# Two unread products behind a LayerNorm, and the Gelu products one V step sooner, in a grouped-query attention and token-mixer decode kernel

## The chip, the cores and the metric

One Trainium2 chip, one of its cores. The metric is the device time of one execution in microseconds; the kernel before has 2511.02 us as the median of three runs (2510.0 to 2511.93).

## The reference, cut to what matters

Two layers, each an attention block over a key/value cache and then a token mixer with a hidden width of 1792 for one token. Batch 2, 8 key/value heads with 4 query heads each, 32768 cached positions of 128 values, model width 512, all in float32. Both layers read the same caches and the same weights, so the caches (1.06 GB for the two layers, less what is kept on chip) pass through the core twice.

```
x = x + A(layernorm(x))      # q = x @ wq; softmax(q k^T * Dh**-0.5) v; @ wo
x = x + B(layernorm(x))      # gelu(h outer w1 + b1) contracted with w2, + b2
x = x + A(layernorm(x))
x = x + B(layernorm(x))
```

In `B` the layernorm's 512 values each meet 1792 hidden units: `u[d, f] = gelu(h[d] * w1[f] + b1[f])`, `y[d] = sum over f of u[d, f] * w2[f] + b2`. The hidden units lie as 14 tiles of 128 partitions by 512 columns.

## The kernel before, in words

**Units and steps.** A unit is (layer, batch, key/value head); there are 32. A unit has a K phase (scores) and a V phase (weighted sum), each of 64 groups of 512 columns, which are worked off four at a time: 16 steps a phase, 1024 steps in all, numbered from 0 in the order that `Order` writes out by hand. A group of the cache fills one of 106 cells of 128 x 512 float32 (256 KB) in SBUF. A step is four matmuls of 128 x 512 into four column strips of one PSUM bank (`k_step` L335, `v_step` L388).

**Hooks.** Everything else is hung on a step: `at(p, f, ...)` (L698) puts a function behind step p, and the loop at the end emits step, hooks, then the loads that may begin after that step. Each engine runs its instructions in the order emitted. So the order of the work on TensorE is written out by hand, and what a hook waits for holds up the V or K steps emitted behind it.

**Loads.** `plan_loads` (L113) decides, from the steps' order and from the microseconds that the hooks are said to take (`us=`, summed by step in `busy`), which cells each load fills, how many groups it has, and the step after which it is issued. All loads go through the queue of SyncE (`load`, L807). A load waits for the steps that last read its cells.

**The change of layer.** A unit of layer 1 needs x after the mixer of layer 0 of its batch. For batch 0 the last unit of layer 0 is x0 = (0, 0, 7), followed in V order by a filler unit of the other batch; then comes y0 = (1, 0, 7), the first unit of layer 1, whose V cells are x0's, still on chip (all 64), with the first 10 groups of K. Batch 1 does the same later with (0, 1, 7), a filler, and (1, 1, 7). While 64 + 10 cells are kept, the filler's V is streamed through 16 cells: four loads of four cells, in turn. Each of them is issued when the step four before it has been worked off.

Behind the last V step of such a unit, called e (e = 463 for the first change, 559 for the second), stand:

- e, e+1: the sum of the heads (`out_1`, `out_2`), `take_rows`
- e+2: `mix_2` (L485, residual into one bank; LayerNorm on VectorE and GpSimd, L492 to L497), `half_way` (`columns`, L552, and L558), ScalarE's table for Gelu
- e+4 to e+11: `hidden_tiles(key, k)` for k = 0 to 7 (L515). Call k first has TensorE multiply the two Gelu tiles of call k-1 (`project`, L507), then ScalarE make tiles 2k and 2k+1 (L522). Of the two tile buffers each is used again only when its product is done.
- e+11: `take_rows` (L465); e+12: `change_1` (x of the new layer, wide query products L300, sum for the mean L546, query row copied by ScalarE L574); e+13: `change_2` (sum of squares L546, power on GpSimd L580, narrow query products L307)
- e+16: the last V step of the filler, then K of the new unit

A third place with the same list, without `half_way`, `change_1` and `change_2`, is the last unit of batch 0 in layer 1, (1, 0, 0), at e = 975, where the steps behind e are K steps. There `mix_4` (L533) follows, which also issues the output's DMA from ScalarE.

**The end.** The last unit, (1, 1, 0), has a tail of its own (`last_rows`, `last_mixer`), with products of TensorE that nobody reads: `unread(n, count)` (L591) multiplies a column of ones with n columns of the tile S into a PSUM bank of the pool `pmisc`. `pmisc` has two banks, in turn used by all small products (`misc` in the profile). A tile of a pool keeps its bank until the last instruction in the program that touches the tile.

Of the kernel before, what the change touches and what calls it, by code (L numbers as in the profile page):

```python
# [13 lines left out]
P = 128  # L14
G = 512
# [180 lines left out]
def gqa_mixer_kernel(ctx: ExitStack, tc: tile.TileContext, x, kt, v, wqo, cols, out):  # L196
    nc = tc.nc
# [5 lines left out]
    FT = (cols.shape[1] - 1) // 3  # L203
# [3 lines left out]
    order = Order(HKV)  # L207
# [14 lines left out]
    def cells(a, n):  # L222
        return mem[:, a * G : (a + n) * G]
# [5 lines left out]
    ident = const.tile([P, P], F32, name="ident")  # L229
    one = const.tile([P, 1], F32, name="one")  # L230
# [7 lines left out]
    S = [const.tile([P, G], F32, name=f"S{k}") for k in range(2)]  # L238
# [349 lines left out]
    rest = [None, None]  # L588
    idle = []

    def unread(n, count=1):  # L591

        if not idle:
            idle.append(pmisc.tile([P, G], F32, name="misc"))
        for _ in range(count):
            nc.tensor.matmul(idle[0][:1, :n], one, S[0][:, :n], start=True, stop=True)  # L596

    def last_rows(u):
        layer, b, h = u
# [13 lines left out]
    def last_mixer(u):  # L613
        layer, b, h = u
        key = (layer, b)
        w = D // 2
        tiles = [cells(tail_at + k, 1) for k in range(TAIL_CELLS)]
        flat, y, few = tiles[FT + 1], tiles[FT + 2], tiles[FT + 3][:, :DH]
        p = px[key]
        st = work.tile([P, 6], F32, name="ln_st")  # L620
        mv = work.tile([P, 2], F32, name="ln_mv")
        rs = work.tile([P, 1], F32, name="ln_rs")
        nc.vector.tensor_copy(few, thin[:, :DH])
        asb["thin"] = few
        out_1(u)
        for k in range(2):
            for r in range(R):
                nc.tensor.matmul(  # L628
                    rest[k][32 * r : 32 * r + 1, :w],
                    oT[u][:, r : r + 1],  # L630
                    wo_of(u)[:, r, k * w : (k + 1) * w],
                    start=True,
                    stop=True,
                )
        unread(P)
        nc.vector.tensor_copy(y[:, :w], rest[0][:, :w])
        nc.scalar.activation(y[:, w:], rest[1][:, :w], AF.Copy)
        nc.tensor.matmul(p, sel1, y, start=False, stop=True, skip_group_check=True)  # L638
        nc.vector.bn_stats(st, p)  # L639
        res = rows[b][:, :P]  # L640
        for g in range(NG):
            nc.tensor.matmul(
                rows[b][32 * g : 32 * g + 1, :P],
                selg[:, 0:1],
                y[:, g * P : (g + 1) * P],
                start=False,
                stop=False,
                skip_group_check=True,
            )
        unread(G, 2)  # L650
        nc.vector.bn_aggr(mv, st)
        deviation(rs, mv)
        off = work.tile([P, 1], F32, name="off", bufs=1)
        nc.vector.tensor_scalar_mul(off, mv[:, 0:1], -1.0)
        nc.vector.tensor_copy(flat, p)
        scale = work.tile([P, FT], F32, name="scale", bufs=1)
        bias = work.tile([P, FT], F32, name="bias", bufs=1)
        nc.vector.tensor_scalar_mul(scale, w1c, rs)
        nc.vector.scalar_tensor_tensor(bias, scale, off, b1c, op0=ALU.mult, op1=ALU.add)

        def project_last(f):
            for g in range(NG):
                nc.tensor.matmul(  # L663
                    rows[b][32 * g : 32 * g + 1, :P],
                    w2c[:, f : f + 1],
                    tiles[f][:, g * P : (g + 1) * P],
                    start=False,
                    stop=(f == FT - 1),
                    skip_group_check=True,
                )  # L670

        for f in range(DIRECT):
            nc.scalar.activation(  # L673
                tiles[f], flat, AF.Gelu_apprx_tanh, bias=bias[:, f : f + 1], scale=scale[:, f : f + 1]
            )
            project_last(f)
            unread(P)
        f0 = DIRECT
        for m in TAIL_GROUPS:
            for f in range(f0, f0 + m):  # L680
                nc.vector.tensor_scalar(
                    tiles[f], flat, scale[:, f : f + 1], bias[:, f : f + 1], op0=ALU.mult, op1=ALU.add
                )
            t = cells(tail_at + f0, m)
            nc.scalar.activation(t, t, AF.Gelu_apprx_tanh)  # L685
            for f in range(f0, f0 + m):
                project_last(f)
            if m == max(TAIL_GROUPS):
                unread(P)
            f0 += m  # L690
        assert f0 == FT
        o = tiles[FT][:, :P]
        nc.vector.tensor_scalar_add(o, res, b2c)
        nc.sync.dma_start(out[b : b + 1, :].rearrange("o (g c) -> (o g) c", g=NG), o[0 : P : P // NG, :])
# [16 lines left out]
    for u in order.units:  # L711
        layer, b, h = u
# [5 lines left out]
        us = (u, mate) if b == 0 and mate not in made and (layer == 0 or h < HKV - 2) else (u,)  # L718
# [5 lines left out]
    for name, us in users.items():  # L724
        k0 = min(first["K", u] for u in us)
        h = name if isinstance(name, int) else name[1]
        layer = min(u[0] for u in us)
        weights.append((k0 - 24 if k0 else -1, (layer, h), max(end["V", u, 1] for u in us) + 3))

    for u in order.units:  # L730
        layer, b, h = u
        key = (layer, b)
        k_mid, k_end = end["K", u, 0], end["K", u, 1]
        v0, v_mid, v_end = first["V", u], end["V", u, 0], end["V", u, 1]
        ahead = order.v_before[u]
# [12 lines left out]
        at(v0 - 1 if u == order.last else v_mid + 2, denominators, u, us=0.4)  # L748
        if u == order.last:
            at(v0 - 1, take_rows, key)  # L750
            at(v0 - 1, table, AF.Gelu_apprx_tanh)
            at(v0 - 1, mix_1, key)
            at(v0 - 1, last_rows, u)
            at(v_mid, unread, G, 3)
            at(v_mid + 4, unread, P, 2)
            at(v_end - 2, take_out, u)
            at(v_end - 2, unread, G)
            at(v_end - 1, out_sum, u)
            at(v_end, last_mixer, u)
            continue  # L760
        at(v_end, take_out, u)
        if u != order.last_of[key]:
            late = 0 if u == order.v_before[order.last] else 1
            at(v_end + late, out_1, u, us=1.2)
            at(v_end + 2 * late, out_2, u, us=2.0)
            continue
        e = v_end
        at(e - 2, mix_1, key, us=1.2)
        at(e, out_1, u, us=1.9)
        at(e + 1, out_2, u, us=2.0)  # L770
        at(e + 1, take_rows, key)
        at(e + 2, mix_2, key, us=1.2)
        if layer == 0:
            at(e + 2, half_way, key, us=1.0)
        at(e + 2, table, AF.Gelu_apprx_tanh)
        for k in range(FT // 2 + 1):
            at(e + 4 + k, hidden_tiles, key, k, us=1.2)
        e += 4 + FT // 2
        at(e, take_rows, key)
        at(e, table, AF.Exp)  # L780
        if layer == 1:
            at(e + 1, mix_4, key, us=1.2)
            continue
        (y,) = [y for y, (x, _) in changed.items() if x == u]
        at(e + 1, change_1, key, y, us=2.2)
        at(e + 2, change_2, key, y, us=0.8)
        assert e + 2 < first["K", y]
# [86 lines left out]
```

## Time and profile before

| what | value |
|---|---|
| median of three runs | 2511.02 us (2510.0 to 2511.93) |
| the profiled execution's own time | 2512.67 us |
| its span, first to last instruction | 2511.0 us |
| granted TensorE clock, mean | 0.754 |
| bytes read | 1064.33 MB, 424 GB/s over the span |

A row of the timeline gives the start in microseconds from the span's start, the duration, the engine, the line, what is written and read, the shape, the number of records, and in brackets the idle time before it and what ended that. A float32 matmul shows as two records, so a V step of four matmuls is "x8". A row of a table by window gives the window, its length, the busy time of the five engines (with counts), the granted clock of TensorE as a share of full speed, the busy share of the 16 DMA engines and the GB/s moved. A row of a DMA issue by line gives the count, the size and the time from issue to landing.

### The profile page before, as it was taken

The numbers are of one execution on the slowest core, as the hardware profiler recorded it, in microseconds if no ns is written. First come the engines' busy times: TensorE is split into PE (matmuls) and PEld (weight loads), VectorE is DVE, ScalarE is ACT, GpSimd is POOL, SyncE is SP. The second block draws the span as 40 slices with busy tenths as digits, with TensorE's granted clock in tenths as the row PEclk, the third lists the DMA queues.
The fourth block names the chain that finished last, engine by engine and source line by source line (L and its number), as shares of the span: only waits on it lengthen the run. The fifth ranks groups of instructions, "written<-read, shape, count | busy, mean of one in ns | idle before, by whom it ended". The sixth has DMA issues, their size and how long they took to land. (4 is left out here: it accounts for less than half of the span.)

```text
span 2511.0 us, 20944 instructions
## 1 busy us (share of the span) xinstructions
PE 1392.1 (55%) x9580; PEld 395.3 (16%) x9580; DVE 179.7 (7%) x486; ACT 186.2 (7%) x580; POOL 5.1 (0%) x18
## 2 busy tenths in 40 slices
PE   3455555554555545556775775455554545555557
PEld 1111111111111111111121121111111111111112
DVE  1000000000000000000010010000000000000011
ACT  0100000000000000001110100000000000000021
POOL 0000000000000000000000000000000000000000
PEclk9777776777767777778887887777677776677788
DMA  9999999999999999999999999999999999999996
GB/s 418 431 431 428 433 434 432 433 433 434 434 433 424 432 435 433 414 433 420 392 421 427 396 428 429 431 433 433 434 434 433 433 424 441 433 426 434 425 432 275
DMA packets 32641, 1065.68 MB, mean 424 GB/s; under 512 B 3877, under 2 KB 3881, under 8 KB 5034
## 3 DMA queue, kind: packets, MB, share of 16 engines
q1 hardware_dynamic: 32264, 1064.32, 98.8%
q8 instruction: 75, 1.23, 0.2%
q14 instruction: 12, 0.10, 0.0%
q10 hardware_dynamic: 290, 0.03, 0.0%
HBM read 1064.33 MB, written 0.00 MB: 424 GB/s over the span
## 5 line engine op out<-in xcount | busy, mean ns | idle before, releaser
L335 PE MATMUL scores<-mem,qz 128*32 128x512 f32 x4096 | 614.6, 740 | 553.2 <-DMA mem<-in_kt_dram 553.2
L388 PE MATMUL acc<-mem,S 128*16 128x512 f32 x4080 | 591.4, 713 | 534.4 <-DMA mem<-in_v_dram 529.4
L370 ACT ACTIVATE S<-S,neg 128x128 f32<-128x128 f32 x256 | 129.9, 510 | 2242.8 <-DVE S L365 1203.9
L335 PEld LDWEIGHTS scores<-mem,qz 128*32 128x32 f32 x4096 | 138.9, 130 | 963.0 <-issue 487.3
L388 PEld LDWEIGHTS acc<-mem,S 128*16 128x16 f32 x4080 | 125.3, 106 | 855.8 <-issue 776.6
L345 DVE TENSOR_REDUCE mx<-scores 128x1 f32<-128x512 f32 x64 | 44.2, 691 | 851.9 <-PE scores L335 851.9
L427 PEld LDWEIGHTS misc<-selg,row 128*128 128x128 f32 x256 | 48.9, 285 | 48.2 <-issue 36.8
L365 DVE STREAM_TRANSPOSE S<-scores 128x512 f32<-128x512 f32 x64 | 45.4, 710 | 113.7 <-PE acc L388 113.7
L427 PE MATMUL misc<-selg,row 128*128 128x4 f32 x256 | 51.7, 325 | 3.3 <-DVE row L419 3.3
L451 PE MATMUL rows<-mem,oT 128*1 128x512 f32 x248 | 51.6, 921 | 0.3 <-DVE oT L442 0.3
L370 ACT ACTIVATION_READ_ACCUMULATOR S<-S,neg 128x1 f32 x256 | 47.8, 187 | 0.0
L355 DVE TENSOR_REDUCE m<-misc 1x4 f32<-1x128 f32 x32 | 8.9, 279 | 367.1 <-PE misc L353 367.1
L419 DVE COPY row<-acc 128x512 f32<-128x512 f32 x32 | 22.1, 691 | 177.3 <-PE acc L388 177.3
L413 DVE RECIPROCAL rl<-misc 128x4 f32<-128x4 f32 x32 | 5.8, 182 | 367.5 <-PE misc L411 367.5
L442 DVE TENSOR_TENSOR oT<-misc,rl 128x4 f32<-128x4 f32 x32 | 5.2, 161 | 270.6 <-PE misc L427 270.2
L507 PE MATMUL rows<-row,cols_sb 128*1 128x512 f32 x42 | 22.3, 614 | 0.6 <-ACT row L522 0.6
L507 PE MATMUL rows<-hid,cols_sb 128*1 128x512 f32 x42 | 22.3, 613 | 0.0
L411 PEld LDWEIGHTS misc<-both,one 128*128 128x128 f32 x64 | 13.7, 267 | 49.7 <-issue 46.8
L300 PE MATMUL misc<-mem,xw 128*32 128x512 f32 x144 | 19.7, 619 | 2.4 <-DVE xw L276 1.9
L522 ACT ACTIVATE row<-bcast,bias,scale 128x512 f32<-128x512 f32 x21 | 16.3, 777 | 39.2 <-PE rows L507 20.6
L307 PEld LDWEIGHTS misc<-selg,row 128*128 128x128 f32 x128 | 16.3, 199 | 17.7 <-issue 10.1
L307 PE MATMUL misc<-selg,row 128*128 128x2 f32 (+1 forms) x128 | 17.7, 260 | 0.8 <-DVE row L292 0.8
(117 smaller groups left out, 240.8 us busy)
## 6 DMA issues: line engine op xcount, KB each, us to landing
mem<-in_kt_dram SPq DMA_DIRECT2D x23, 2048.0 KB, 14.2
mem<-in_v_dram SPq DMA_DIRECT2D x37, 1024.0 KB, 8.8
mem<-in_kt_dram SPq DMA_DIRECT2D x8, 4096.0 KB, 23.8
mem<-in_wqo_dram SPq DMA_DIRECT2D x14, 2048.0 KB, 33.4
mem<-in_v_dram SPq DMA_DIRECT2D x7, 4096.0 KB, 22.9
mem<-in_v_dram SPq DMA_DIRECT2D x3, 6144.0 KB, 30.0
mem<-in_kt_dram SPq DMA_DIRECT2D x18, 1024.0 KB, 10.7
mem<-in_v_dram SPq DMA_DIRECT2D x6, 2048.0 KB, 26.3
```

Source lines behind the costliest of these rows:

```text
L300: nc.tensor.matmul(q_ps[us][32 * d : 32 * d + 32, :], xw[:, d, :], wq[:, d, :], start=True, stop=True)
L307: nc.tensor.matmul(pt[:, r * n : (r + 1) * n], q_row[us][:, r * DH : (r + 1) * DH], side, start=True, stop=True,)
L335: nc.tensor.matmul(sc_ps[u, half][32 * row : 32 * row + 32, :], qz[:, at : at + 32], cells(at_cell["K", u, g], 1), start=(i == 0), stop=(i ...
L345: nc.vector.tensor_reduce(mx[u][:, half : half + 1], sc_ps[u, half], axis=AX.X, op=ALU.max)
L365: nc.vector.transpose(S[half], sc_ps[u, half])
L370: nc.scalar.activation(s[:, :, h], s[:, :, h], AF.Exp, bias=neg[u][:, h : h + 1], scale=SCALE, accum_out=lsum[u][:, half, h : h + 1],)
L388: nc.tensor.matmul(acc[32 * row : 32 * row + R * QT, :], S[half][:, col : col + R * QT], vc, start=(g < NG), stop=(g >= quads - NG),)
L419: nc.vector.tensor_copy(asb[u], acc)
L427: nc.tensor.matmul(po_of[u][:, :R], asb[u][:, t * DH : (t + 1) * DH], selg[:, t * R : (t + 1) * R], start=(t == 0), stop=(t == QT - 1 and ...
L451: nc.tensor.matmul(rows[b][32 * r : 32 * r + 1, :], oT[u][:, r : r + 1], wo_of(u)[:, r, :], start=(u == order.first_of[layer, b]), stop=(u ...
L507: nc.tensor.matmul(rows[key[1]][32 * g : 32 * g + 1, :], w2c[:, f : f + 1], hid.pop((key, f)), start=(f < NG), stop=(f >= FT - NG),)
L522: nc.scalar.activation(hid[key, f], px[key], AF.Gelu_apprx_tanh, bias=shift[key][:, f : f + 1], scale=slope[key][:, f : f + 1],)
```

## The change

- `unread` gets the unit as its first argument. For a unit other than the last it takes a new `misc` tile each time and multiplies the ones with a broadcast column of the identity matrix in place of S.
- In layer 0 two calls are added: 256 columns behind e+2 (after `mix_2`, `half_way` and the table), 512 columns behind e+3.
- `hidden_tiles(key, k)` moves from step e+4+k to e+3+k, in all three places. All that is counted from there (`take_rows`, the table for Exp, `change_1`, `change_2`, `mix_4`) moves one step forward with it, and so do the entries of `busy` that the planner reads.
- For the last unit, a new tile is taken only when the list `idle` is empty, which it is not any more: the tile of the second change of layer serves again.

```diff
-    def unread(n, count=1):
-
-        if not idle:
+    def unread(u, n, count=1):
+
+        if not idle or u != order.last:
+            idle.clear()
             idle.append(pmisc.tile([P, G], F32, name="misc"))
         for _ in range(count):
-            nc.tensor.matmul(idle[0][:1, :n], one, S[0][:, :n], start=True, stop=True)
+            nc.tensor.matmul(idle[0][:1, :n], one, S[0][:, :n] if u == order.last else ident[:, :1].to_broadcast([P, n]), start=True, stop=True)
...
         at(e + 2, table, AF.Gelu_apprx_tanh)
+        if layer == 0:
+            at(e + 2, unread, u, G // 2)
+            at(e + 3, unread, u, G)
         for k in range(FT // 2 + 1):
-            at(e + 4 + k, hidden_tiles, key, k, us=1.2)
-        e += 4 + FT // 2
+            at(e + 3 + k, hidden_tiles, key, k, us=1.2)
+        e += 3 + FT // 2
         at(e, take_rows, key)
```

The calls of `unread` in the tail pass `u` and are otherwise as they were.

More of the change, by code (lines that the diff above doesn't have):

```diff
@@ L634, in last_mixer @@
                 )
-        unread(P)
+        unread(u, P)
         nc.vector.tensor_copy(y[:, :w], rest[0][:, :w])
@@ L649, in last_mixer @@
             )
-        unread(G, 2)
+        unread(u, G, 2)
         nc.vector.bn_aggr(mv, st)
@@ L676, in last_mixer @@
             project_last(f)
-            unread(P)
+            unread(u, P)
         f0 = DIRECT
@@ L688, in last_mixer @@
             if m == max(TAIL_GROUPS):
-                unread(P)
+                unread(u, P)
             f0 += m
@@ L753, in gqa_mixer_kernel @@
             at(v0 - 1, last_rows, u)
-            at(v_mid, unread, G, 3)
-            at(v_mid + 4, unread, P, 2)
+            at(v_mid, unread, u, G, 3)
+            at(v_mid + 4, unread, u, P, 2)
             at(v_end - 2, take_out, u)
-            at(v_end - 2, unread, G)
+            at(v_end - 2, unread, u, G)
             at(v_end - 1, out_sum, u)
```

## The prediction

> **What bounds the kernel.** I read the page first, then windows around the two changes of layer, then the timeline and the SyncE queue there and at the end.
>
> ```profile
> span 2511.0 us, 20944 instructions
> ...
> q1 hardware_dynamic: 32264, 1064.32, 98.8%
> ...
> L335 PE MATMUL scores<-mem,qz 128*32 128x512 f32 x4096 | 614.6, 740 | 553.2 <-DMA mem<-in_kt_dram 553.2
> L388 PE MATMUL acc<-mem,S 128*16 128x512 f32 x4080 | 591.4, 713 | 534.4 <-DMA mem<-in_v_dram 529.4
> ```
>
> The load queue is busy 98.8% of the span, and TensorE's idle time before K and V steps ends with a landing. So the time is bytes over the queue's rate plus the tail; an edit on TensorE counts only where it makes a load late. At most 1.2% is to be had, and most of that lies in a few places. Two are the ends of the changes of layer (last two columns: DMA share, GB/s):
>
> ```profile
> 1198.00:1210.00 12.00, 10.53 (x74) 3.27 (x66) 1.78 (x8) 5.49 (x8) 0.00 (x0) 1.00 1.01 421
> 1210.00:1222.00 12.00, 10.56 (x81) 3.95 (x80) 1.81 (x8) 0.00 (x0) 0.54 (x1) 0.86 0.87 326
> 1397.00:1409.00 12.00, 9.25 (x65) 3.33 (x65) 2.43 (x12) 4.79 (x7) 0.54 (x1) 1.00 1.01 420
> 1409.00:1421.00 12.00, 11.63 (x87) 3.73 (x86) 1.15 (x4) 0.00 (x0) 0.00 (x0) 0.86 0.89 335
> ```
>
> Against the 12 us before, 12 x (1 - 326/421) = 2.7 us of transfer are missing at the first change and 12 x (1 - 335/420) = 2.4 us at the second: 5.1 us in all, 0.2% of the time. This is also about what a measurement of this kernel can tell from no change.
>
> Why they are missing, at the first change:
>
> ```profile
> 1202.58 1.05 PE L388 MATMUL acc<-mem,S 128*16 128x512 f32 x8 [0.21 <-DMA mem<-in_v_dram]
> ...
> 1205.05 1.05 PE L388 MATMUL acc<-mem,S 128*16 128x512 f32 x8 [0.50 <-DMA mem<-in_v_dram]
> 1206.04 1.05 PE L552 MATMUL misc<-selg,row 128*128 128x1 f32 x8
> 1207.35 1.06 PE L300 MATMUL misc<-mem,xw 128*32 128x512 f32 x8 [0.26 <-DVE xw L566]
> 1208.34 0.38 PE L546 MATMUL misc<-xw,one 128*128 128x4 f32 x2
> 1208.66 1.05 PE L388 MATMUL acc<-mem,S 128*16 128x512 f32 x8
> 1209.64 0.39 PE L546 MATMUL misc<-sq,one 128*128 128x4 f32 x2
> 1211.43 1.15 PE L307 MATMUL misc<-pair,row 128*128 128x1 f32 x8 [1.40 <-DVE pair L584]
> 1212.51 4.27 PE L388 MATMUL acc<-mem,S 128*16 128x512 f32 x24
> ```
>
> Steps e+11 and e+12 come 2.47 us apart, with the landings. `change_1` puts e+13 at 1208.66, `change_2` puts e+14 at 1212.51, though its load landed about 2.5 us before. The queue meanwhile (an issue, then its size and time to landing, from windows around that issue alone):
>
> ```profile
> 1209.77 0.33 SPq L807 DMA_DIRECT2D mem<-in_kt_dram  x1
> mem<-in_kt_dram SPq DMA_DIRECT2D x1, 512.0 KB, 6.4
> 1214.48 0.33 SPq L807 DMA_DIRECT2D mem<-in_kt_dram  x1
> mem<-in_kt_dram SPq DMA_DIRECT2D x1, 1024.0 KB, 6.3
> 1407.06 0.33 SPq L807 DMA_DIRECT2D mem<-in_kt_dram  x1
> mem<-in_kt_dram SPq DMA_DIRECT2D x1, 512.0 KB, 6.4
> 1411.20 0.33 SPq L807 DMA_DIRECT2D mem<-in_kt_dram  x1
> mem<-in_kt_dram SPq DMA_DIRECT2D x1, 1024.0 KB, 5.9
> 1437.29 0.33 SPq L807 DMA_DIRECT2D mem<-in_kt_dram  x1
> mem<-in_kt_dram SPq DMA_DIRECT2D x1, 2048.0 KB, 8.1
> ```
>
> The load behind e+13 has only 2 groups (512 KB), that behind e+14 has 4. The second is issued at 1214.48, 1.97 us after e+14 began, and lands at 1220.8, the one ahead of it at 1216.2: 4.6 us for 2.47 us of data, 2.2 us lost. A late load takes 6.3 - 2.5 = 3.8, 5.9 - 2.5 = 3.4 or 8.1 - 4.9 = 3.2 us beyond its data (0.61 us a group). I call this the lead: a load is in time when issued some 3.5 us before the load ahead of it lands.
>
> **The change, part by part.**
>
> *Unread products.* The nearest row is the tail's own:
>
> ```profile
> 2479.23 2.74 PE L596 MATMUL misc<-S,one 128*1 128x512 f32 x6
> 1185.00:1188.00 3.00, 2.22 (x12) 0.29 (x16) 0.00 (x0) 0.00 (x0) 0.00 (x0) 0.50 1.00 415
> ```
>
> Three of 512 columns take 2.74 us, so 0.9 us one, 0.45 us one of 256, twice that at half clock: 1.4 to 2.7 us of TensorE at each change. The steps e+3 to e+5 wait for landings, and a load there may be issued over 3 us late before the queue runs dry, since four loads circulate (4 x 2.47 less the lead and a step). Cost 0; were that cover gone, up to 2.7 us. The window shows half clock there before the change, with the DMA share at 1.00: what the products may do to the clock is worth 0 as well.
>
> *Products one step sooner.* Call 0's two Gelu tiles follow the LayerNorm at once in either version, since ScalarE does not wait for TensorE there; the products follow e+4 in place of e+5. From then on each call keeps pace with the landings, so `take_rows`, `change_1` and `change_2` come 2.47 us sooner. The moved steps issue no load and change no order on the SyncE queue; GpSimd's power and the Exp table go with them, with nothing of other units in between. The output's DMA of `mix_4` moves one K step, in a stage where the queue is full.
>
> `change_2` does not get shorter: what it delays is now e+13 in place of e+14. First change: e+13 at 1212.51 - 2.47 = 1210.04, its 512 KB load issued 1.97 us later at 1212.0. The load ahead of it, the filler's last, lands at 1206.17 + 8.8 = 1215.0 now, and does so still, though it is issued about 1 us later behind a later e+12:
>
> ```profile
> 1206.17 0.33 SPq L807 DMA_DIRECT2D mem<-in_v_dram  x1
> mem<-in_v_dram SPq DMA_DIRECT2D x1, 1024.0 KB, 8.8
> ```
>
> The lead is 3.0 us, so 0.5 us is lost, and some 0.4 us by the load after it. Against 2.2 us (2.7 us with what trails) the gain is 1.3 us; I take **-1.5**, between -2.7 and 0.
>
> Second change, where the chain has one wait more. `misc` has two banks, but the tile taken behind e+3 here is used again in the tail, so its bank is held from here to the end and all small products share one:
>
> ```profile
> 1404.63 1.06 PE L300 MATMUL misc<-mem,xw 128*32 128x512 f32 x8 [0.26 <-DVE xw L566]
> 1405.63 0.38 PE L546 MATMUL misc<-xw,one 128*128 128x4 f32 x2
> 1405.77 0.60 ACT L574 ACTIVATE row<-misc 128x512 f32<-128x512 f32 x1 [3.50 <-PE misc L300]
> 1409.67 4.46 PE L388 MATMUL acc<-mem,S 128*16 128x512 f32 x24
> ```
>
> L546's sum stood beside L300's bank; now it waits until ScalarE has copied that at 1406.37: 0.7 us on `change_1`, and step e+12 and `change_2` behind it on TensorE. In the rest of layer 1 each small product begins after the reader of the one before has ended, so nothing is added. Step e+13 then starts at 1409.67 - 2.47 + 0.7 = 1407.9, its load goes out 1.5 us later (1411.20 - 1409.67) at 1409.4. The load ahead lands at 1407.06 + 6.4 - 1.2 = 1412.2 (two groups before the one issued at 1407.06): a lead of 2.8 us, so 0.7 us lost and 0.5 us by the next. That is 1.2 us, and 1.2 us is lost there now (1411.20 + 5.9 = 1417.1 against 1413.5 + 2.47). I take **-0.2**, between -2.4 and +0.7.
>
> Both use the half clock at which these steps run now (0.86 granted in both windows). At full clock the releases come 0.9 us sooner and both changes gain about 1 us more. By the Trainium skill ("TensorE: Matmul & The Clock Gate", "Part 1: The HAM clock gate (the "warmup" mystery)") the clock is halved after an idle window of some 3.4 us that runs free of the kernel's start. By that rule an execution may meet either clock here, and the sum would lie up to 2 us lower; the trace shows half clock at both, so the sum keeps it.
>
> *The planner.* Its list, worked through with the shifted entries, is the same for 213 loads, both changes of layer included, and differs at the end, through the third place (e = 975). Groups, and the step after which they are issued:
>
> | | before | after |
> |---|---|---|
> | V of (1,1,1) | 0-23: 981, 24-31: 983, 32-63: 990 | 0-23: 975, 24-31: 983, 32-55: 983, 56-63: 999 |
> | V of the last unit | 0-15 and 16-31: 999, 32-47: 1007, rest: 1011 | 0-15: 1000, 16-31: 1006, 32-47: 1011, rest: 1015 |
>
> The first half of this gets earlier, the second half later: one step 1000, one 1006, then a step four later for all that is left.
>
> ```profile
> 2425.10 0.33 SPq L807 DMA_DIRECT2D mem<-in_v_dram  x1
> mem<-in_v_dram SPq DMA_DIRECT2D x1, 27.7
> 2452.84 3.61 PE L388 MATMUL acc<-mem,S 128*16 128x512 f32 x16 [16.54 <-DMA mem<-in_v_dram]
> 2472.36 1.06 PE L388 MATMUL acc<-mem,S 128*16 128x512 f32 x8
> 2476.04 0.33 SPq L807 DMA_DIRECT2D mem<-in_v_dram  x1
> ```
>
> Now the load of 32 groups lands at 2452.8, and step 1000 starts on it. With 24 groups that is 8 x 0.61 = 4.9 us sooner, 2447.9; the step at half clock ends near 2449.9 (two take 3.61), and the load behind it is issued at 2450.0, 2.8 us ahead of the landing of the last 8 groups: 0.7 us late. The stage up to step 1008 is 4.9 us sooner too (2467.5), step 1011's load is issued 3.7 us after that (2476.04 - 2472.36) at 2471.2, while the load ahead lands at 2452.8 + 0.7 + 32 x 0.61 = 2473.0: a lead of 1.8 us, 1.7 us late. The rest is in time. Together 2.4 us; the bounds are 0 and 4.5 us: with 3.8 us of lead the two cost 1.0 + 2.0, and if part of steps 1008 to 1011 ran at half clock, 1.5 us more. Some may be made up in the last 64 groups; I take **+2.0**, nearer to the rows than either end.
>
> *Sum:* -1.5 - 0.2 + 2.0 = +0.3 us. The profiled execution (2512.67 us, span 2511.0) lies 1.65 us over the median; the sum is a difference and is laid on the median: **2511.3 us**.
>
> **The rivals.**
>
> *The queue stays full.* If 2 us of lead are enough, none of the loads above is late but the one behind 1011, by 0.2 us (2.0 - 1.8): both shortfalls go and the end costs nothing, 2511.0 - 5.1 + 0.2 = 2506.1, or 2507.8 if only the late loads' own 2.2 + 1.2 us return. For it: 1215.0 - 1212.0 = 3.0 is not far from 3.2. Against it: the load at 1411.20 was issued 2.3 us ahead of the landing at 1413.5 and still lost 1.2. Chance 0.2. The Trainium skill ("SBUF — State Buffer", "The DMA setup-cost knee (why "@ 1 MiB" ≠ asymptote)") gives a transfer a fixed cost of about 2 us; by that the time would be this rival's, and the three late loads above do not agree with it.
>
> *Slower: the last loads.* The place is steps 1000 to 1015. If steps 1008 to 1011 run at half clock (two in 3.61 us, so 7.2 us in place of 3.7), the load behind 1011 goes out at 2474.7, after the one ahead has landed: 5.3 us late, +6.0 at the end, and with nothing gained at the changes 2517.0. It decides from about 2.7 us of delay in that stage on. Against it: the stage is at full clock now, right from 2472. Chance 0.12.
>
> *It does nothing.* The stalls move by one step and the late loads at the end are made up: 2511.0. Chance 0.13; the forecast has 0.55.
>
> **The numbers.** The range reaches to the better half of the first rival, 2507.5, and to 2515.0, where +4.5 at the end meets small gains. Faster by over 0.2% (under 2506.0) needs both shortfalls whole: 0.05. Slower by over 0.2% (over 2516.0): 0.08. The rest, 0.87, is the same.
>
> **What would show it.** Step e+13 in place of e+14 should follow L307; at the second change L546 should start as L574 ends. The windows after 1210 and 1409 should show 350 to 400 GB/s. In the last 60 us there should be a dip of the DMA share near 2452 and 2473, and the last landing near 2493 to 2495. Wrong would be: another plan of loads, a full share at the end, or a landing lead under 2.5 us.

## The result, and the profile after

The changed kernel takes 2514.89 us (median of 13 runs, 2512.39 to 2520.6). Beside it, the kernel before had 2508.85 us (median of 13 runs, 2504.36 to 2511.93). The ratio is 1.0025 with a 95% interval of 1.0017 to 1.0032, so the changed kernel is 6.0 us slower. The forecast was 2511.3 us, 0.3 us more than before and no change that can be told. The time lies inside the stated range of 2507.5 to 2515.0 us, but only by luck: the range was laid on 2511.02 us, and the kernel before was 2.2 us faster in these runs. Taken as differences from before, the range was -3.5 to +4.0 us, and the measured +6.0 us lies outside it.

One thing has to be known for all that follows. The execution profiled before took 2512.67 us, which is 3.8 us above the median of these 13 runs; the one profiled after took 2514.98 us, which is its median. A single profile shows where a wait is; the ratios over many runs say what it is worth. One thousandth is 2.5 us.

The page of the changed kernel, the lines that answer to those shown of before:

```profile
span 2513.3 us, 20953 instructions
...
q1 hardware_dynamic: 32408, 1064.32, 98.8%
...
L335 PE MATMUL scores<-mem,qz 128*32 128x512 f32 x4096 | 612.0, 737 | 555.4 <-DMA mem<-in_kt_dram 555.3
L388 PE MATMUL acc<-mem,S 128*16 128x512 f32 x4080 | 601.2, 721 | 521.2 <-DMA mem<-in_v_dram 516.4
```

The bound is the same: the load queue moves the same bytes and is busy 98.8% of a longer span. TensorE's V products take 601.2 us against 591.4 at the same count and its K products 612.0 against 614.6; the clock granted over the whole span is 0.754 in both, so the clock has to be looked at place by place. The table by window at the two changes of layer (the last three columns: granted clock, DMA share, GB/s):

```profile
1198.00:1210.00 12.00, 8.95 (x65) 3.51 (x60) 2.51 (x13) 3.73 (x6) 0.54 (x1) 1.00 1.01 423
1210.00:1222.00 12.00, 11.09 (x84) 3.17 (x83) 1.16 (x4) 0.00 (x0) 0.00 (x0) 0.86 0.95 346
1397.00:1409.00 12.00, 9.71 (x52) 4.48 (x56) 2.06 (x13) 0.60 (x1) 0.54 (x1) 0.59 0.85 343
1409.00:1421.00 12.00, 10.57 (x80) 3.04 (x76) 0.85 (x2) 0.00 (x0) 0.00 (x0) 0.84 0.79 279
```

At the first change the shortfall is a little smaller than before (346 GB/s for 326). At the second it spreads over both windows: 12 x (1 - 343/421) + 12 x (1 - 279/421) = 2.2 + 4.0 = 6.3 us of transfer are missing, where before it was 2.4. And TensorE has a clock of 0.59 there, in a window in which it had 1.00.

The timeline of the second change in the changed kernel shows why. Two rows of before come first, for comparison: the filler's sum of its two halves on VectorE (L410) and its product on TensorE (L411).

```profile
1382.03 0.15 DVE L410 TENSOR_TENSOR both<-lsum 128x4 f32<-128x4 f32 x1
1399.26 0.38 PE L411 MATMUL misc<-both,one 128*128 128x4 f32 x2
```

```profile
1395.80 0.69 DVE L465 COPY row<-rows 128x512 f32<-128x512 f32 x1 [16.31 <-PE rows L507]
1396.40 0.15 DVE L410 TENSOR_TENSOR both<-lsum 128x4 f32<-128x4 f32 x1
1396.61 0.38 PE L411 MATMUL misc<-both,one 128*128 128x4 f32 x2 [0.89 <-DVE both L410]
1396.93 1.05 PE L388 MATMUL acc<-mem,S 128*16 128x512 f32 x8
...
1399.22 1.94 PE L300 MATMUL misc<-mem,xw 128*32 128x512 f32 x8 [0.26 <-DVE xw L566]
1401.22 0.60 ACT L574 ACTIVATE row<-misc 128x512 f32<-128x512 f32 x1 [5.29 <-PE misc L300]
1401.87 0.59 PE L546 MATMUL misc<-xw,one 128*128 128x4 f32 x2 [0.72 <-ACT row L574]
1402.39 1.91 PE L388 MATMUL acc<-mem,S 128*16 128x512 f32 x8
...
1406.14 1.86 PE L307 MATMUL misc<-pair,row 128*128 128x1 f32 x8 [1.31 <-DVE pair L584]
1407.93 6.01 PE L388 MATMUL acc<-mem,S 128*16 128x512 f32 x32
```

Three things are to be seen.

- **A new wait, 0.89 us.** Before, VectorE did L410 at 1382.03, long ahead, and L411 ran without a wait. Now L410 stands behind the copy of `take_rows` (L465), which itself waited for the last Gelu product. TensorE waits for L410, and the V step of 1396.93 stands behind L411 on TensorE.
- **The held bank, 0.72 us.** L546 waits for ScalarE's copy (L574), as the prediction had it.
- **The clock.** L300, which took 1.06 us before, takes 1.94, and the V step and L307 behind it are as slow (1.91 and 1.86). Before, the whole chain ran at full clock and only the steps behind it at half. The slow stretch begins at L300, behind the wait of 0.89 us and ahead of that of 0.72 us, so in this execution the held bank did not bring it on.

The loads show what this did to the queue. The filler's last V load is issued behind the V step of 1402.39, at 1404.36, and lands 4.6 us later, at 1408.9 (its rows stand in the last section). The next one, the K load of 512 KB behind step e+13, is issued here:

```profile
1409.90 0.33 SPq L811 DMA_DIRECT2D mem<-in_kt_dram  x1
```

That is 1.0 us after the load ahead of it has landed. The prediction had it 2.8 us ahead of that landing.

At the end of the kernel, the window that holds the first late load, the late load itself, and the two waits of TensorE for the last V loads:

```profile
2448.00:2452.00 4.00, 2.63 (x16) 0.49 (x16) 0.00 (x0) 0.00 (x0) 0.00 (x0) 0.50 0.55 233
```

```profile
2451.34 0.33 SPq L811 DMA_DIRECT2D mem<-in_v_dram  x1
...
2472.02 0.33 SPq L811 DMA_DIRECT2D mem<-in_v_dram  x1
mem<-in_v_dram SPq DMA_DIRECT2D x1, 4096.0 KB, 13.1
```

```profile
2474.61 5.15 PE L388 MATMUL acc<-mem,S 128*16 128x512 f32 x32 [2.63 <-DMA mem<-in_v_dram]
...
2485.28 4.94 PE L388 MATMUL acc<-mem,S 128*16 128x512 f32 x32 [2.95 <-DMA mem<-in_v_dram]
```

The load behind step 1011 goes out at 2472.02, 2.6 us ahead of the landing (2474.61, where TensorE's wait ends) of the load in front of it, and takes 13.1 us. The plan of loads is the one that was forecast.

### The profile page after: what moved, and what is told of

The parts are those of the page before. It is cut to its first block, busy times and chain, and to the rows that moved or that the text cites. A ratio compares the mean times of both kernels' runs of the same rounds, so it can differ in the third digit from the quotient of the medians.

```text
span 2513.3 us, 20953 instructions
## 1 busy us (share of the span) xinstructions
PE 1401.5 (56%) x9588; PEld 399.0 (16%) x9588; DVE 179.8 (7%) x486; ACT 186.1 (7%) x580; POOL 5.1 (0%) x18
## 3 DMA queue, kind: packets, MB, share of 16 engines
q1 hardware_dynamic: 32408, 1064.32, 98.8%
## 5 line engine op out<-in xcount | busy, mean ns | idle before, releaser
L335 PE MATMUL scores<-mem,qz 128*32 128x512 f32 x4096 | 612.0, 737 | 555.4 <-DMA mem<-in_kt_dram 555.3
L388 PE MATMUL acc<-mem,S 128*16 128x512 f32 x4080 | 601.2, 721 | 521.2 <-DMA mem<-in_v_dram 516.4
L300 PE MATMUL misc<-mem,xw 128*32 128x512 f32 x144 | 20.5, 645 | 2.4 <-DVE xw L276 1.9
L411 PEld LDWEIGHTS misc<-both,one 128*128 128x128 f32 x64 | 13.6, 265 | 51.2 <-issue 43.9
L307 PEld LDWEIGHTS misc<-selg,row 128*128 128x128 f32 x128 | 16.3, 200 | 19.0 <-issue 8.5
L411 PE MATMUL misc<-both,one 128*128 128x4 f32 x64 | 16.4, 326 | 3.7 <-DVE both L410 3.7
```

The lines of the kernel that those rows point to most:

```text
L300: nc.tensor.matmul(q_ps[us][32 * d : 32 * d + 32, :], xw[:, d, :], wq[:, d, :], start=True, stop=True)
L307: nc.tensor.matmul(pt[:, r * n : (r + 1) * n], q_row[us][:, r * DH : (r + 1) * DH], side, start=True, stop=True,)
L335: nc.tensor.matmul(sc_ps[u, half][32 * row : 32 * row + 32, :], qz[:, at : at + 32], cells(at_cell["K", u, g], 1), start=(i == 0), stop=(i ...
L388: nc.tensor.matmul(acc[32 * row : 32 * row + R * QT, :], S[half][:, col : col + R * QT], vc, start=(g < NG), stop=(g >= quads - NG),)
L411: nc.tensor.matmul(pl[:, :R], ones, both, start=True, stop=True)
```

## The experiments

Each result is the ratio to the kernel before that was measured beside it, with its 95% interval. The intervals are 0.0008 to 0.0013 to either side, so most differences between two kernels lie within them; what is read from such a difference rests on its coming out twice and on the profiles.

The change has five parts that can be set apart: the unread products; the bank that their tile keeps to the end; the earlier products in layer 0; the order on VectorE that comes with them; and the third place, in layer 1, whose only effect on the loads is another plan for the end. The first four kernels take the change apart roughly, the next four one part each.

**e1_move_only.** The products one step sooner in all three places, no unread products ahead of the Gelu tiles; both banks stay free. The cut is against the kernel before.

```diff
-            at(e + 4 + k, hidden_tiles, key, k, us=1.2)
-        e += 4 + FT // 2
+            at(e + 3 + k, hidden_tiles, key, k, us=1.2)
+        e += 3 + FT // 2
```

> The products come one step sooner in all three places, without the two unread products at the changes; the tail takes its own tile, so two banks serve the small products throughout. If the move itself costs (the copy of the rows now stands ahead of the filler's denominators on VectorE, TensorE waits for them at step e+10, and the change runs at half clock): 4 to 6 us over before, like the changed kernel. If the bank held from the second change on is the cost: within 1.5 us of before. If the plan of the last loads is the cost: 1 to 2.5 us over before.

Measured: 1.0034 (1.0021 to 1.0047), from six runs. The move alone, without held bank and without unread products, is slower than before, by 8.5 us and so by more than the 4 to 6 us that were expected.

**e2_unread_only.** The changed kernel with the products at their old steps: unread products and held bank are left.

```diff
-            at(e + 3 + k, hidden_tiles, key, k, us=1.2)
-        e += 3 + FT // 2
+            at(e + 4 + k, hidden_tiles, key, k, us=1.2)
+        e += 4 + FT // 2
```

> The two unread products and the tile reused in the tail, with the Gelu products at their old steps; the plan of loads is that of before. If the move costs: within 1.5 us of before. If the held bank costs: 0.7 us or more at the second change, in all 1 to 4 us over before. If the plan of the last loads costs: as before.

Measured: 1.0010 (1.0002 to 1.0019). So the other half of the change has a cost too.

**e3_fresh_tile.** The changed kernel, whose tail takes a tile of its own, so that no bank is held.

```diff
-        if not idle or u != order.last:
+        if not idle or u != order.last or idle[-1] is None:
             idle.clear()
...
+        if u != order.last:
+            idle[-1] = None
```

> The changed kernel, but the tail takes a tile of its own, so that two banks serve the small products of layer 1. If the held bank is the cost: back within 1.5 us of before, with the sum of L546 starting right behind L300 at the second change. If the move or the plan is the cost: still 4 to 6 us over before, at most 1 us better than the changed kernel.

Measured: 1.0021 (1.0012 to 1.0029), against 1.0025 with the held bank. The intervals overlap; by itself this pair decides nothing.

**e4_layer1_old.** The changed kernel with the third place at its old steps, hence the old plan of loads.

```diff
+        late = 3 + layer
         for k in range(FT // 2 + 1):
-            at(e + 3 + k, hidden_tiles, key, k, us=1.2)
-        e += 3 + FT // 2
+            at(e + late + k, hidden_tiles, key, k, us=1.2)
+        e += late + FT // 2
```

> The changed kernel, but the third place (layer 1) stays at its old steps, so the last loads are planned as before. If the plan of the last loads is the cost: 1 to 2.5 us better than the changed kernel, the last landing 1 us or more sooner against the loads before step 975. If the second change is the cost: 3.5 to 5 us over before.

Measured: 1.0015 (1.0006 to 1.0023). The two changes of layer alone, forecast as a gain of 1.7 us, are a loss of 3.8 us.

**f1_denominators_sooner and f2_layer0_two_banks.** f2 is e4 with the tail's own tile (as in e3): earlier products in layer 0, unread products, two banks, old plan. f1 is f2 with the fillers' `denominators` put one step sooner, so that L410 stands ahead of L465 on VectorE again.

```diff
-        at(v0 - 1 if u == order.last else v_mid + 2, denominators, u, us=0.4)
+        at(v0 - 1 if u == order.last else v_mid + (1 if u in [f for _, f, _ in order.changes] else 2), denominators, u, us=0.4)
```

> Changes of layer 0 as in the changed kernel, but with two banks throughout, the last loads planned as before, and the filler's denominators one step sooner (behind e+9), so that VectorE has them before it copies the rows. If the wait for that copy is what eats the gain of the moved products: the small sum L411 waits for nothing, the change's products stand a whole step (2.47 us) sooner against the landings, the load behind the narrow query products is in time, and the time is 1 to 4 us under before. If the clock is the cause: as the kernel without this edit, and half clock inside the change.

> The same without the edit of the denominators: the two changes alone, with two banks and the old plan. If the held bank and the plan of the last loads make up the loss of the changed kernel: within 1.5 us of before. If the wait for the copy or the clock costs by itself: 1.5 to 4 us over before.

Measured: f2 1.0009 (1.0000 to 1.0017), f1 0.9998 (0.9989 to 1.0007). One edit in the order of two hooks is worth 0.0011, 2.8 us; the two intervals overlap, and g2 below repeats the pair. The wait came out as expected, the time did not: f1 is 0.5 us under before, where 1 to 4 us were expected. The timeline of f1 at the second change, where everything lies some 2 us earlier than in the changed kernel:

```profile
1391.08 0.39 PE L411 MATMUL misc<-both,one 128*128 128x4 f32 x2
...
1393.69 0.69 DVE L465 COPY row<-rows 128x512 f32<-128x512 f32 x1 [2.01 <-PE rows L507]
1394.20 1.05 PE L388 MATMUL acc<-mem,S 128*16 128x512 f32 x8 [0.54 <-DMA mem<-in_v_dram]
```

The V step waits for its landing again, not for VectorE, and the sequence of f1 is the one that the prediction had drawn.

**f3_layer1_only.** The kernel before with the third place alone moved: only the plan of the last loads differs.

```diff
+        late = 4 - layer
         for k in range(FT // 2 + 1):
-            at(e + 4 + k, hidden_tiles, key, k, us=1.2)
-        e += 4 + FT // 2
+            at(e + late + k, hidden_tiles, key, k, us=1.2)
+        e += late + FT // 2
```

> The kernel before with the third place alone moved, so that only the plan of the last loads differs. If two late loads and a slower clock behind them cost at the end: 2 to 4 us over before, with the last landing 1 us or more later against the loads before step 975, and the load behind step 1011 late. If the plan is harmless: within 1 us of before.

Measured: 1.0012 (1.0003 to 1.0020), 3.0 us. The medians differ by less, 2510.34 against 2509.33 us, so the size is uncertain. The wait for the late load in the timeline of before, and then the two in f3's, whose profiled execution was the slowest of its runs (2517.68 us):

```profile
2483.25 3.63 PE L388 MATMUL acc<-mem,S 128*16 128x512 f32 x32 [1.28 <-DMA mem<-in_v_dram]
```

```profile
2475.17 5.09 PE L388 MATMUL acc<-mem,S 128*16 128x512 f32 x32 [2.75 <-DMA mem<-in_v_dram]
2486.85 6.07 PE L388 MATMUL acc<-mem,S 128*16 128x512 f32 x32 [4.03 <-DMA mem<-in_v_dram]
```

The profiles of all kernels support the 3 us. From the landing of the last of the 213 loads that both plans share (it brings K groups) to the end of the span, the profiled executions of the eleven kernels with the old plan have 96.4 us on average (95.7 to 97.8), the six with the new plan 99.6 (97.9 to 102.0).

**f4_unread_two_banks.** The unread products alone, as in e2, but with the tail's own tile as in e3: no bank is held.

> The two unread products alone, with two banks and every product at its old step. If the held bank is what the kernel with the unread products alone lost (2.5 us): back to within 1 us of before. If the products themselves cost: 1.5 to 3 us over before still.

Measured: 1.0000 (0.9992 to 1.0009). Here the unread products are free, and against e2's 1.0010 the held bank costs 0.0010. By f2 and e4, where it is the same pair with the products moved, it costs 0.0006, and by e3 and the changed kernel 0.0004. No pair by itself sets it apart from nothing; all three have the same sign. The timeline of e2 shows what goes with it:

```profile
1401.57 1.06 PE L300 MATMUL misc<-mem,xw 128*32 128x512 f32 x8 [0.26 <-DVE xw L566]
1403.35 0.38 PE L546 MATMUL misc<-xw,one 128*128 128x4 f32 x2 [0.72 <-ACT row L574]
1403.67 1.91 PE L388 MATMUL acc<-mem,S 128*16 128x512 f32 x8
```

The V step right behind the wait of 0.72 us is slow, where L300 ahead of it was not. It is so in e2, e4 and g2 (1.91, 1.91 and 1.69 us), the three kernels whose bank is held and whose L300 took 1.06 us; in the ten kernels with two banks and L300 at 1.06 or 1.07 us, the same V step took 1.05 us.

**g1_sooner_no_unread.** f1 without the unread products ahead of the Gelu tiles.

```diff
-        if layer == 0:
-            at(e + 2, unread, u, G // 2)
-            at(e + 3, unread, u, G)
```

> The kernel with the products of layer 0's change one step sooner, the denominators one step sooner too and two banks, with the unread products at the changes left out (the ratio to before was 0.9998 with them). If the unread products are worth nothing, the ratio is again 0.9998 within 0.0008. If they hold TensorE's clock through the change, the half clock comes into the change more often and the ratio is 1.0002 to 1.0010 (1 to 3 us slower than with them). If they only cost TensorE's time, it is 0.9990 to 0.9996.

Measured: 1.0000 (0.9991 to 1.0009), against 0.9998. Where they were put, the unread products neither cost nor gain anything that these runs can tell.

**g2_changed_den_sooner and g4_before_den_sooner.** The `denominators` one step sooner, once in the changed kernel as the only edit (the diff of f1), once in the kernel before.

> The changed kernel with one edit: the filler's denominators are put one step sooner, so that VectorE adds the two halves ahead of the copies of take_rows. Theory of the order on VectorE: the ratio falls from 1.0025 by the 0.0011 that this edit was worth without the held bank, to 1.0014 (2512.4 us), and the stretch from the landing of the load two steps ahead of the change's last step to the sum of squares shortens by some 0.8 us at both changes. What stays is the held bank (0.0006) and the plan of the last loads (0.0012). Rival, that the lost time is in the held bank and the plan alone: 1.0025 within 0.0005.

> The kernel before with one edit: the filler's denominators one step sooner. There the add of the two halves ran long ahead of the copies of take_rows, so by the theory of the order on VectorE the edit has nothing to gain: the ratio is 1.0000 within 0.0004. If the earlier denominators are worth something by themselves, wherever the products stand, it is 0.9989 as between the two kernels with the sooner products.

Measured: g2 1.0014 (1.0005 to 1.0023), g4 1.0001 (0.9991 to 1.0012). The edit takes 0.0011 off the changed kernel and nothing off the kernel before, where L410 had no copy ahead of it. That is what the theory of the order on VectorE says. The pair of f1 and f2 gave the same 0.0011.

**g3_unread_in_change.** f1 with one unread product more, of 512 columns, in `change_2` where TensorE waits for GpSimd's power, at both changes.

```diff
         all_sum(spread, sq)
+        unread(y, G)
         nc.vector.tensor_scalar(spread, spread, 1.0 / D, EPS, op0=ALU.mult, op1=ALU.add)
```

> The kernel with the products of layer 0's change and the denominators one step sooner and two banks (ratio 0.9998), plus one unread product of 512 columns in change_2 behind the sum of squares. If a halved clock inside the change is what is left of the time there, this holds it and the ratio is 0.9990 to 0.9996 (0.5 to 2 us less). If the clock's pieces come from the wait ahead of that point, the added product changes nothing: 0.9998 within 0.0005. If it only delays the broadcast behind it, 1.0000 to 1.0004.

Measured: 0.9990 (0.9980 to 1.0000), at the edge of what can be told.

**h1_changed_den_fill and h3_unread_held_fill.** The held bank was forecast at 0.7 us of delay and measured at 1.0 to 2.5 us. To see whether the rest is the clock, g2 (h1) and e2 (h3) get two unread products inside the second change, written into the held bank itself: the bank stays held and L546 still waits for ScalarE, but TensorE is idle for less of that time.

```diff
+    def fill(b, n):
+        if b == 1:
+            nc.tensor.matmul(idle[0][:1, :n], one, ident[:, :1].to_broadcast([P, n]), start=True, stop=True)
...
         wide_products(us, wq_sb[0, y[2]])
+        fill(b, G // 2)
         all_sum(negm, x)
...
         all_sum(spread, sq)
+        fill(b, G)
```

> The changed kernel with the denominators one step sooner (ratio 1.0014), its bank held as there, and at the second change one unread product of 256 columns behind the wide query products, where TensorE waits some 0.7 us for ScalarE's copy, and one of 512 behind the sum of squares, where it waits 1.4 us for the power. Both go into the held bank. Theory that the held bank costs its 0.8 us and through the clock some 2 us more: the stretch at half clock of 10 us that begins inside the second change is gone or shortened to 3 to 7 us behind the change, and the ratio falls to 1.0004 to 1.0009. Rival, that the wait alone costs: the clock may change, the ratio stays at 1.0014 within 0.0004.

> The kernel with the unread products and the held bank but the Gelu products at their old steps (ratio 1.0010), with the same two unread products inside the second change. Theory of the clock: 1.0002 to 1.0005, and no stretch at half clock of over 7 us begins inside the second change. Rival, that the wait alone costs: 1.0010 within 0.0004.

Measured: h1 1.0003 (0.9992 to 1.0013) where g2 has 1.0014; h3 1.0001 (0.9992 to 1.0010) where e2 has 1.0010. The windows of the second change, of g2 and then of h1:

```profile
1397.00:1409.00 12.00, 9.71 (x54) 4.17 (x57) 1.87 (x12) 0.60 (x1) 0.54 (x1) 0.63 0.81 309
1409.00:1421.00 12.00, 9.48 (x76) 2.75 (x72) 0.85 (x2) 0.00 (x0) 0.00 (x0) 0.93 0.96 375
```

```profile
1397.00:1409.00 12.00, 10.52 (x76) 3.69 (x72) 2.56 (x13) 1.74 (x3) 0.55 (x1) 1.00 0.97 384
1409.00:1421.00 12.00, 8.91 (x76) 2.56 (x72) 0.85 (x2) 0.00 (x0) 0.00 (x0) 1.00 1.00 411
```

And e2, then h3, in the same windows:

```profile
1397.00:1409.00 12.00, 9.21 (x56) 4.05 (x48) 2.25 (x11) 2.79 (x5) 0.54 (x1) 0.78 0.95 385
1409.00:1421.00 12.00, 11.62 (x82) 3.44 (x81) 1.15 (x4) 0.00 (x0) 0.00 (x0) 0.80 0.75 294
```

```profile
1397.00:1409.00 12.00, 10.36 (x68) 3.33 (x60) 2.44 (x12) 4.18 (x6) 0.54 (x1) 1.00 1.01 421
1409.00:1421.00 12.00, 10.26 (x88) 3.54 (x87) 1.15 (x4) 0.00 (x0) 0.00 (x0) 1.00 0.90 358
```

With more work on TensorE inside the change, the clock is 1.00 in both windows and the queue keeps 0.97 and more of its share in the first. The timeline of h1 shows that the bank is still held (L546 behind ScalarE's copy, here L575) and the idle time shorter, 0.30 us for the 0.72 in the changed kernel:

```profile
1401.44 0.60 PE L595 MATMUL misc<-ident,one 128*1 128x256 f32 x2
1401.69 0.60 ACT L575 ACTIVATE row<-misc 128x512 f32<-128x512 f32 x1 [3.54 <-PE misc L300]
1402.34 0.38 PE L546 MATMUL misc<-xw,one 128*128 128x4 f32 x2 [0.30 <-ACT row L575]
1402.65 1.05 PE L388 MATMUL acc<-mem,S 128*16 128x512 f32 x8
```

Each pair of intervals overlaps; both pairs and their profiles point the same way, and both gains are a little more than was expected. From the start of L300 to L546 nothing is shortened: it is 1.78 us in h1 (1400.56 to 1402.34) and 1.78 us in e2 (1401.57 to 1403.35). What differs is the V step behind, 1.05 us in h1. So the gain of some 0.001 is put down to the clock. How much of it answers the held bank isn't shown: the second product, of 512 columns, stands in a wait that is there with two banks too, and there such products, put in at both changes, bring 0.0008 (g3 against f1) and 0.0013 (h2 below against g1). The first product alone was not tried.

**h2_only_in_change.** g3 without the unread products ahead of the Gelu tiles.

> The kernel with the products and the denominators one step sooner and one unread product of 512 columns in change_2 (ratio 0.9990), without the unread products ahead of the Gelu tiles, which were worth nothing elsewhere. If the gain comes from the product inside the change alone, the ratio is again 0.9990 within 0.0008. If it needs both, it is 0.9998 to 1.0002.

Measured: 2506.36 us, 0.9987 (0.9978 to 0.9996). It has the products one step sooner in layer 0, the denominators one step sooner, and one unread product in `change_2`. This is the one kernel of all whose whole interval is under 1; out of so many kernels that alone would be weak, but g3's 0.9990 supports it. Against 421 GB/s, its windows at the two changes lack 1.4 us of transfer, where before lacks 5.1:

```profile
1198.00:1210.00 12.00, 10.68 (x76) 4.00 (x71) 2.70 (x14) 3.84 (x6) 0.54 (x1) 1.00 1.01 417
1210.00:1222.00 12.00, 9.80 (x76) 2.75 (x72) 0.90 (x3) 0.00 (x0) 0.00 (x0) 0.86 0.99 391
1397.00:1409.00 12.00, 9.18 (x70) 3.17 (x74) 1.87 (x12) 0.60 (x1) 0.55 (x1) 1.00 1.00 406
1409.00:1421.00 12.00, 8.96 (x72) 2.42 (x64) 0.85 (x2) 0.00 (x0) 0.00 (x0) 0.94 1.02 421
```

## Why the prediction was wrong, step by step

The parts as the runs have them, beside the terms of the sum:

| part | forecast, us | measured (ratio x 2509) | from |
|---|---|---|---|
| unread products ahead of the Gelu tiles | 0 | 0 | f4, g1 against f1 |
| products one step sooner in layer 0 | -1.5 and -0.2, the held bank within | +2.3 | f2 |
| of this, the order on VectorE | not seen | +2.8 | f2 - f1, after - g2 |
| held bank | 0.7 of delay, within the -0.2 | +1.0 to +2.5 | after - e3, e4 - f2, e2 - f4 |
| plan of the last loads | +2.0 | +2.5 to +3.0 | after - e4; f3, e3 - f2 |
| whole | +0.3 | +6.3 (+6.0 by the medians) | after; the parts are 2.3 + 1.5 + 3.0 = 6.8 |

Each difference of two ratios is uncertain by about 0.0012, 3 us, so the parts are rough sizes.

**The step that failed** is the sentence that the moved steps go "with nothing of other units in between". The terms of -1.5 and -0.2 us for the two changes of layer rest on it; e4 has +3.8 us in their place. The filler's `denominators` are hung on its v_mid + 2, which is e+10, the very step to which `take_rows` moved, and there `take_rows` is emitted first. In the kernel before, VectorE came to L410 with nothing ahead of it and did it 17 us early; so the trace showed no wait. The prediction named SyncE's queue, GpSimd's power and ScalarE's table in that place and did not ask what VectorE had at that step. The price is a wait of 0.85 to 0.89 us on TensorE at each change, in place of one of 0.2 us for the landing, so the chain came about 0.7 us later than the 2.47 us sooner that I took as given. Two changes make 1.4 us; the runs have 2.8 (f2 against f1, the changed kernel against g2; together an estimate of 0.0011 within 0.0009, worked out from the four intervals). In what is left the clock has a part. Five kernels have this wait, at both changes: after, e1, e3, e4 and f2. In four of these ten places L300 behind it is slow, 1.59 to 1.94 us. One is the first change of e4, ahead of any held bank:

```profile
1200.72 0.39 PE L411 MATMUL misc<-both,one 128*128 128x4 f32 x2 [0.85 <-DVE both L410]
...
1203.33 1.93 PE L300 MATMUL misc<-mem,xw 128*32 128x512 f32 x8 [0.26 <-DVE xw L566]
```

In the 24 places without this wait L300 takes 1.06 or 1.07 us. What the slow clock behind this wait costs was not measured by itself.

**The gain at the changes** was read from late loads in one execution that was 3.8 us above the median. With the order put right, f1 gives 0.9998 (0.9989 to 1.0007): -0.5 us, where -1.7 was forecast for both changes; the interval holds both, and nothing. The shortfalls do shrink in its profile: the four windows at the changes have 408, 384, 398 and 413 GB/s, which is 2.3 us of transfer missing against 421, where before lacks 5.1. With an unread product in TensorE's wait as well (h2) 1.4 us are missing, and the time is 3.3 us under before.

**The held bank** had its mechanism and place right: L546 begins as L574 ends, as the prediction said it would. What failed is the size. I counted 0.7 us of waiting and kept the clock of the kernel before; 1.0 to 2.5 us were measured. In the three profiled executions in which the chain is at full clock up to this wait and nothing fills it, TensorE was granted 0.63, 0.68 and 0.78 in the window 1397 to 1409 (g2, e4, e2); before had 1.00. (In the changed kernel's 0.59 the clock had fallen ahead of it, at L300.) At half clock the same chain takes nearly twice its time on TensorE: V step 1.91 for 1.05 us, L307 1.87 (e2) for 1.02. In h1 and h3 the bank is held too and the clock stays. The Trainium skill ("TensorE: Matmul & The Clock Gate", "Part 1: The HAM clock gate (the "warmup" mystery)") has TensorE's clock halved after an idle window of about 3.4 us. In these runs no wait of TensorE in the chain was longer than 1.4 us, and the clock fell all the same; 1.6 us more of work was enough to have 1.00 in h1 where g2 has 0.63. The prediction had used that rule only for a gain of up to 2 us; the clock came out as a loss.

**The plan of the last loads** came as forecast, with its two late loads, and cost 2.5 to 3.0 us for 2.0, inside the bounds of 0 and 4.5. The load behind step 1000 was issued at 2451.34; the one ahead of it at 2439.38, and landed 14.8 us later:

```profile
mem<-in_v_dram SPq DMA_DIRECT2D x1, 2048.0 KB, 14.8
```

That is a lead of 2.8 us, as worked out. From that landing (2454.2) to the landing that step 1008 waited for (2474.6) are 20.4 us for 32 x 0.61 = 19.5 us of data: 0.9 us late, 0.7 forecast. The second had a lead of 2.6 us (1.8 forecast) and took 2485.3 - 2474.6 = 10.7 us for 9.8: 0.9 late, 1.7 forecast. Together that is 1.8 us, less than the 2.4 us forecast for the loads, so some 1 us arises elsewhere. Where is not shown; in both f3 and the changed kernel the steps behind the second late load took longer (6.07 and 4.94 us against 3.63 before). The 1.5 us for a slow clock, which the upper bound had, stood for steps 1008 to 1011, not for these.

**The rivals.** "The queue stays full" needs loads that are in time with 2 us of lead. The two late loads at the end, with 2.8 and 2.6 us, each lost 0.9 us, which speaks against it; one load at the second change speaks for it (last section), but the one behind that was issued too late for either rule. "Slower: the last loads" had the right place for half of the loss, at +3.0 and not +6.0. That other costs, as large together, would stand at the changes themselves, where I had put only gains, was in no rival: the chances of a loss were taken from the end alone. Among the signs named, e+13 in place of e+14 behind L307, L546 at L574's end, and the dip near 2452 (233 GB/s) came, and the last landing near 2493 to 2495 nearly (2495.4); 350 to 400 GB/s behind both changes did not (346 and 279).

**Left open:** e1 (1.0034, six runs) against e3 (1.0021), which differ in the unread products alone; the intervals overlap, and between f1 and g1, with the order put right, there is a difference of 0.0002 the other way. How the cost of the held bank divides between its 0.7 us and the clock is open as well.

## What to carry to other kernels

When a hook is moved by a step, write down for every engine, VectorE too, what else is hung on the step that it moves to, and in which order: an instruction that ran far ahead without a wait shows nothing in the trace until something late is put in front of it. A wait on TensorE inside a chain that sets the end of a stage can cost more than its own length: look whether the clock is still granted there, and if it is not, try filling the wait with products nobody reads. In this kernel an unread product helped where TensorE waits inside the chain, not some eight steps ahead of it, and its tile must not be one that a later stage uses again.

## What was not expected of the hardware

- A wait of 0.7 us cost 1.0 to 2.5 us by three pairs of kernels, and the V step right behind it took 1.69 to 1.91 us in place of 1.05. With 1.6 us of unread products (0.60 and 1.02) in it and in the next wait, 0.001 of the time came back, and the clock over 12 us went from 0.63 to 1.00.
- The lead that a load needs isn't one number. I had 3.2 to 3.8 us from loads of before. In the changed kernel a V load of four groups, issued 1.8 us ahead of the landing of the one in front, landed 4.6 us after its issue, 2.1 us beyond its 2.47 us of data:

```profile
1404.36 0.33 SPq L811 DMA_DIRECT2D mem<-in_v_dram  x1
mem<-in_v_dram SPq DMA_DIRECT2D x1, 1024.0 KB, 4.6
```

The Trainium skill ("SBUF — State Buffer", "The DMA setup-cost knee (why "@ 1 MiB" ≠ asymptote)") has about 2 us of fixed cost for a transfer; this load agrees with it, the load of 13.1 us for 9.8 us of data doesn't, with 3.3. What sets them apart wasn't tried.
